# Reading x by column-tiled matmuls at the head of the second state visit, in an attention and gated FFN kernel

## The chip, the cores and the metric

The kernel runs on one core of a Trainium2 chip. The metric is the device time of one execution in microseconds (us). The core has a matrix engine (TensorE, PE in the profile, its weight loads PEld), a vector engine (VectorE, DVE), a scalar engine (ScalarE, ACT), a general one (GpSimd, POOL) and one that issues DMAs (SyncE, SP). Each takes its own list of instructions in order; they wait for each other by semaphores.

## The reference

There are 8 batches of 8 heads. In each head x has 512 rows and the state 32 rows, of 64 columns. x reads the state by softmax attention, and the state reads x; both results stand one under the other, and the 544 rows of a batch (heads side by side, 512 columns) go through a feed-forward layer with a gate.

```python
scores = scale * np.matmul(x, state.transpose(0, 1, 3, 2))
a = softmax(scores)                      # over the 32 state rows
xread = np.matmul(a, state)
scores2 = scale * np.matmul(state, x.transpose(0, 1, 3, 2))
a2 = softmax(scores2)                    # over the 512 rows of x
sread = np.matmul(a2, x)
x = np.concatenate([xread, sread], axis=2)       # to (8 * 544, 512)
gate = 1.0 / (1.0 + np.exp(-(x @ w_gate)))       # 512 -> 1536
out = (gate * (x @ w_val)) @ w_out               # 1536 -> 512
```

## The kernel before, in words

Everything is written out in order by hand (manual_schedule): an instruction stands in its engine's list where its call stands in the code. Matrices are bf16, sums float32.

For the rows of x the kernel doesn't form xread. It multiplies the state with the gate and value weights first (sw_wide, with sw_mm at L272: 64x32 tiles of the array, results in PSUM, copied to the tile SW by sw_cp at L310), and then multiplies the normalised attention (aT) with SW (gv_mm, L324). One batch has 12 steps f. Each step does four 512-column matmuls in gv_mm (two for the gate in one PSUM bank, two for the value in another), the tanh of the gate on ACT (gv_th, L334), the product of both on DVE (gv_glu, L339), and four matmuls of the output product of the batch before (out_mm, L355; every third ends a block, which ACT copies to res, L359, and SP writes out, L363).

The loop from L685 runs over b from 2 to 8. While batch b is in its gv_mm, the attention of batch nb = b + 1 is prepared, in the holes between:

- steps 0 and 6 (the two state visits, v = 0 and 1): sw_wide makes half of SW. Its first two results go to the banks OU (the output product's) and AT (the attention's), four more to the pool SWP. Then stands gv_mm of the step, then out_mm; in the other steps out_mm stands first;
- steps 1 and 2: S_mm (L136), the scores, into AT; S_exp (L141), their exponential E1, on ACT;
- steps 2 and 4: n_sum (L154, L156), the row sums and their reciprocals; steps 5 and 6: n_mul (L208), the attention product ab; step 6: aT_dma (L229), four transposing DMAs on SP's queue;
- step 3: at_Eb (L147), E1 as bf16 (Eb) on POOL; n_add (L173, L174) on DVE and p_fold (L182 to L193) on POOL, which add E1 up over the rows of x into hl;
- steps 9 and 10: the state reads x. sr_mm multiplies hl with the constant matrix pick (L241), which gives the sums, and then x with Eb: 16 matmuls (L249) with 128 columns of x (two heads) as weights and 64 columns of Eb moving. Half of the product (one head with the other's attention) isn't used. sr_inv (L254) takes the reciprocal of the sums on DVE, sr_fin (L262) multiplies and writes the columns of batch nb of XS;
- load_x (L75) for nb + 2 at step 0, cast_x (L99, POOL) and at_xT_dma (L123, SP) for nb + 1 at step 2. For nb = 3 some of it stands at steps 3 and 6.

The last pass, b = 8, multiplies the 256 rows in XS with the weights (L327) as batch 8. Batches 0 to 2 have their attention ahead of the loop, at L438 to L683, written out call by call, with sr_mm as above.

The pools for PSUM: AT one bank, OU one, GV two (gate and value, in turn), SWP four.

Of the kernel before, what the change touches and what calls it, by code (L numbers as in the profile page):

```python
# [8 lines left out]
FP = mybir.dt.float32  # L9
BF = mybir.dt.bfloat16  # L10
AF = mybir.ActivationFunctionType
ALU = mybir.AluOpType
# [4 lines left out]
def kernel(  # L17
# [14 lines left out]
    nc = tc.nc  # L32
    B, H, S, D = x.shape
    Ns = state.shape[2]
# [8 lines left out]
    wp = ctx.enter_context(tc.tile_pool(name="wp", bufs=1))  # L43
    stg = ctx.enter_context(tc.tile_pool(name="stg", bufs=3))
    xp = ctx.enter_context(tc.tile_pool(name="xp", bufs=2))
    ap_ = ctx.enter_context(tc.tile_pool(name="ap", bufs=2))
# [12 lines left out]
    wg = wp.tile((128, 4, dff), BF, name="wg")  # L59
    wv = wp.tile((128, 4, dff), BF, name="wv")  # L60
    wo = wp.tile((128, NF, 512), BF, name="wo")
    sTd = wp.tile((128, 2, H, 2, Ns), BF, name="sTd")
    XS = wp.tile((128, 4, B * Ns), BF, name="XS")

    AT, OU, GV, SWP = (p_at, "at"), (p_out, "outp"), (p_gv, "gv"), (p_sw, "swp")
    xfs, xhs, xbs, xTs = {}, {}, {}, {}
# [21 lines left out]
    def gate(landed):  # L88

        nc.gpsimd.tensor_copy(pre[:, 1:2], landed)  # L90
# [61 lines left out]
    def n_sum(b, i):  # L152
        rs = ap_.tile((128, 8, 2), FP, name="rs")
        nc.vector.tensor_reduce(rs, halfE(b, i), AX.X, ALU.add)  # L154
        ri = held["ri", b, i] = ap_.tile((128, 8, 2), FP, name="ri")
        nc.vector.reciprocal(ri, rs)  # L156
# [12 lines left out]
    def n_add(b):  # L169

        E2 = ap_.tile((128, 2, 2, 4, Ns), FP, name="E2", bufs=1)
        held["E4", b] = ap_.tile((128, 2, 4, Ns), FP, name="E4")
        nc.vector.tensor_tensor(E2, E1s[b][:, 0:2], E1s[b][:, 2:4], ALU.add)  # L173
        nc.vector.tensor_tensor(held["E4", b], E2[:, 0], E2[:, 1], ALU.add)  # L174
# [29 lines left out]
    def n_mul(b, i, eng, lo=0, n=4):  # L204
        if b not in abs_:
            abs_[b] = ap_.tile((128, 4, 2, 128), BF, name="ab")
        ri, ce = held["ri", b, i], slice(2 * lo, 2 * lo + 2 * n)
        eng.tensor_tensor(abs_[b].rearrange("p c e (j n) -> p (c e) j n", n=Ns)[:, ce, 2 * i:2 * i + 2],  # L208
                          halfE(b, i)[:, ce], ri[:, ce].unsqueeze(3).to_broadcast((128, 2 * n, 2, Ns)), ALU.mult)
# [26 lines left out]
    def sr_mm(b, place):  # L236
        Eb = Ebs[b]
        held["sr", b] = place[0].tile((128, 512), FP, name="srp", tag=place[1])
        sr, sm = sr_parts(b)
        if ("hl", b) in held:  # L240
            nc.tensor.matmul(sm, pick, held["hl", b], start=True, stop=True)  # L241
            terms = []
        else:
            terms = [(e, Eb[:, c, e]) for e in range(2) for c in range(4)]
        for i, (e, rhs) in enumerate(terms):
            nc.tensor.matmul(sm, ones[:, e], rhs, start=(i == 0), stop=(i == len(terms) - 1))
        for j in range(4):
            for c in range(4):
                nc.tensor.matmul(sr[:, j], xbs[b][:, c, 2 * j:2 * j + 2].rearrange("p h d -> p (h d)"),  # L249
                                 Eb[:, c, :, j], start=(c == 0), stop=(c == 3))  # L250

    def sr_inv(b):
        r2 = held["r2", b] = ap_.tile((128, 4, Ns), FP, name="r2")
        nc.vector.reciprocal(r2, sr_parts(b)[1])  # L254

    def sr_fin(b):
        if ("r2", b) not in held:
            sr_inv(b)
        sr, r2 = sr_parts(b)[0], held["r2", b]
        for e in range(2):  # L260
            rows = slice(e * 64, (e + 1) * 64)
            nc.vector.tensor_tensor(XS[rows, :, b * Ns:(b + 1) * Ns], sr[rows, :, e], r2[rows], ALU.mult)  # L262

    sw_left = {}

# [20 lines left out]
            for e in range(2):  # L288
                sw_left[b, lo, w, e] = (SWs[b][:, e, w, lo:lo + n], pss[e])

    def sw_wide(b, v):

        if b not in SWs:
            SWs[b] = fp.tile((128, 2, 2, dff), BF, name="SW", bufs=2)
        lo = 768 * v
        for k, places in enumerate(((OU, AT), (SWP, SWP), (SWP, SWP))):
            pss = [p[0].tile((128, 512), FP, name="swp", tag=p[1]) for p in places]
            if k < 2:
                sw_mm(pss, b, k, lo, 512, 0)
            else:  # L300
                for w in range(2):
                    sw_mm(pss, b, w, lo + 512, 256, 256 * w)
            for e in range(2):
                if k < 2:
                    sw_left[b, v, k, e] = (SWs[b][:, e, k, lo:lo + 512], pss[e])
                else:
                    sw_left[b, v, k, e] = (SWs[b][:, e, :, lo + 512:lo + 768], pss[e].rearrange("p (w n) -> p w n", w=2))

    def sw_cp(b, lo, w, e, cp):
        cp(*sw_left.pop((b, lo, w, e)))  # L310
# [5 lines left out]
    def gv_mm(b, f, place):  # L316
        n = n_of(b)
        fs = slice(f * 128, (f + 1) * 128)
        pss = []
        for w in range(2):  # L320
            ps = place[0].tile((128, 512), FP, name="gvp", tag=place[1])[:, :n]
            if b < B:
                for g in range(2):
                    nc.tensor.matmul(ps, SWs[b][:, g, w, fs], aTs[b][:, :, g], start=(g == 0), stop=(g == 1))  # L324
            else:
                for j in range(4):
                    nc.tensor.matmul(ps, (wg, wv)[w][:, j, fs], XS[:, j], start=(j == 0), stop=(j == 3))  # L327
            pss.append(ps)
        held["gv", b, f] = pss

# [15 lines left out]
    def out_mm(b, k, place=None):  # L346
        c, f0 = k // 3, (k % 3) * 4
        if b == 0:

            c, f0 = k // 6 * 2 + k % 2, k % 6 // 2 * 4  # L350
        if f0 == 0:
            place = place or (SWP if b == B else OU)
            ops[b, c] = place[0].tile((128, 512), FP, name="outp", tag=place[1])
        for f in range(f0, f0 + 4):
            nc.tensor.matmul(ops[b, c], glus[b][:, f, c * 128:(c + 1) * 128], wo[:, f],  # L355
                             start=(f == 0), stop=(f == NF - 1))
        if f0 == 8:
            res = fp.tile((128, 512), FP, name="res", bufs=4)
            nc.scalar.activation(res, ops[b, c], AF.Copy, scale=0.5)  # L359
            if b < B:  # L360
                n = 256 if b == B - 2 and c < 3 else 512
                for lo in range(0, 512, n):
                    nc.sync.dma_start(rows_of(b, c)[:, lo:lo + n], res[:, lo:lo + n])  # L363
            else:
                for i in range(4):
                    r0 = (4 * c + i) * SC + S
                    eng = nc.gpsimd if c == 1 and i > 1 else nc.sync
                    eng.dma_start(out[r0:r0 + Ns], res[i * Ns:(i + 1) * Ns])  # L368
# [313 lines left out]
    gate(xTs[2][:, 0, 3, 0:1])  # L682
    gv_glu(1, 5)  # L683

    for b in range(2, B + 1):  # L685
        nb = b + 1 if b + 1 < B else None
        for f in range(NF):

            v, q = divmod(f, 6)
            ahead = nb is not None and q == 0  # L690
            if ahead:
                sw_wide(nb, v)
                sw_cp(nb, v, 0, 0, act)
                sw_cp(nb, v, 0, 1, act)
            for first in (ahead, not ahead):
                if first:
                    gv_mm(b, f, SWP if b == B and f % 2 else GV)
                    gv_th(b, f)
                    gv_glu(b, f)
                elif b < B or f < 9:  # L700
                    out_mm(b - 1, f)
            if nb is not None:
                if f in (0, 8):
                    sw_cp(nb, v, 1, 0, vec)
                if q in (1, 3, 4):
                    k = max(q + 1, 3)
                    sw_cp(nb, v, k // 2, k % 2, act)
                if f in (1, 2):
                    S_mm(nb, f - 1, AT)
                    S_exp(nb, f - 1)  # L710
                elif f == 9:
                    sr_mm(nb, AT)
                    sr_inv(nb)
                elif f == 10:
                    sr_fin(nb)
                if f in (2, 4):
                    n_sum(nb, f // 2 - 1)
                elif f in (5, 6):
                    n_mul(nb, f - 5, nc.vector)
                if f == 3:  # L720
                    n_add(nb)
                    at_Eb(nb)
                    p_fold(nb)
                if f == (3 if nb == 3 else 0) and nb + 2 < B:
                    load_x(nb + 2, nc.sync)
                if f == 6:
                    aT_dma(nb)
                if f == (6 if nb == 3 else 2) and nb + 1 < B:
                    cast_x(nb + 1, pool, 0, 4)
                    cast_x(nb + 1, pool, 4, 4)  # L730
                    at_xT_dma(nb + 1)
# [33 lines left out]
```

## Time and profile before

| | |
|---|---|
| median of 3 runs | 225.42 us (224.99 to 225.9) |
| profiled execution | 224.94 us |
| its span | 223.2 us |
| mean granted TensorE clock | 0.999 |
| PE, share of the span | 97% |
| DVE | 60% |
| ACT | 58% |
| POOL | 35% |

The profile is one execution. Its parts are the busy time of each engine, the span in 40 slices, the chain of work that ended last (followed back from the last instruction to what released each step), and groups of instructions by line, with mean duration and the idle time before them. The trace behind it gives instructions in order of time: start, time that the group took, engine, line, operation, tiles, tile of the array where there is one (64*32), shape, count, and in brackets the idle time before it and who ended it. Durations of matmuls include their way through the array, so neighbours overlap; the distance between starts tells what each costs.

### The profile page before, as it was taken

The numbers are of one execution on the slowest core, as the hardware profiler recorded it, in microseconds if no ns is written. First come the engines' busy times: TensorE is split into PE (matmuls) and PEld (weight loads), VectorE is DVE, ScalarE is ACT, GpSimd is POOL, SyncE is SP. The second block draws the span as 40 slices with busy tenths as digits, with TensorE's granted clock in tenths as the row PEclk, the third lists the DMA queues.
The fourth block names the chain that finished last, engine by engine and source line by source line (L and its number), as shares of the span: only waits on it lengthen the run. The fifth ranks groups of instructions, "written<-read, shape, count | busy, mean of one in ns | idle before, by whom it ended". The sixth has DMA issues, their size and how long they took to land.

```text
span 223.2 us, 4814 instructions
## 1 busy us (share of the span) xinstructions
PE 215.4 (97%) x1843; PEld 109.9 (49%) x1843; DVE 133.2 (60%) x229; ACT 129.5 (58%) x243; POOL 79.1 (35%) x166
## 2 busy tenths in 40 slices
PE   8688999999999999999999999999999999999994
PEld 8553344544444544444545444445445444566843
DVE  3799897967476646765485558563857344322301
ACT  2598886269675557556765658476665444432410
POOL 7987487650048502821262316400560000000001
PEclk9999999999999999999999999999999999999999
DMA  6999999916693269425551315230122112111113
GB/s 97 180 205 264 228 179 169 264 39 167 148 345 109 59 162 263 119 55 167 182 122 37 106 53 113 56 101 13 47 73 71 48 56 68 69 47 50 47 38 103
DMA packets 38871, 26.32 MB, mean 118 GB/s; under 512 B 21089, under 2 KB 34529, under 8 KB 38849
## 3 DMA queue, kind: packets, MB, share of 16 engines
q1 hardware_dynamic: 29600, 17.64, 30.3%
q0 software_dynamic: 8960, 8.19, 21.1%
q8 instruction: 14, 0.23, 0.4%
q10 hardware_dynamic: 288, 0.20, 0.3%
q14 instruction: 9, 0.07, 0.1%
HBM read 18.35 MB, written 8.91 MB: 122 GB/s over the span
## 4 chain that ended last, share of the span: by engine, by line
PE 92%; DVE 6%; ACT 1%; issue 0%; DVEq 0%
PE outp L355 38%; PE gvp L324 36%; PE swp L272 5%; PE gvp L327 5%; PE warm L391 2%; PE srp L249 1%; PE Sp L136 1%; PE outp L377 1%; DVE ab L208 1%; DVE ab L166 1%; DVE glu L339 1%; DVE rs L154 1%; PE aTp L215 1%; DVE rs L160 1%; DVE xT L118 0%; PE stp L413 0%
## 5 line engine op out<-in xcount | busy, mean ns | idle before, releaser
L339 DVE SCALAR_TENSOR_TENSOR glu<-th,gvp 128x512 bf16<-128x512 f32 (+1 forms) x108 | 70.1, 657 | 70.8 <-ACT th L334 55.4
L355 PE MATMUL outp<-wo,glu 128*128 128x512 bf16 x396 | 98.1, 379 | 0.0
L324 PE MATMUL gvp<-aT,SW 128*128 128x512 bf16 x384 | 96.8, 379 | 0.1
L334 ACT ACTIVATE th<-gvp 128x512 f32<-128x512 f32 (+1 forms) x108 | 61.6, 576 | 59.2 <-PE gvp L324 48.2
L324 PEld LDWEIGHTS <-SW 128*128 128x128 bf16 x384 | 36.1, 98 | 45.0 <-issue 4.1
L355 PEld LDWEIGHTS <-glu 128*128 128x128 bf16 x396 | 37.5, 98 | 41.0 <-issue 0.4
L310 ACT CAST SW<-swp 128x512 bf16<-128x512 f32 x74 | 40.9, 586 | 3.5 <-PE swp L272 2.2
L147 POOL CAST Eb<-E 128x256 bf16<-128x256 f32 x32 | 11.6, 410 | 56.0 <-ACT E L141 56.0
L359 ACT ACTIVATE res<-outp 128x512 f32<-128x512 f32 x33 | 19.7, 598 | 18.3 <-PE outp L355 18.2
L368 POOL DMA_DIRECT2D out_dram<-res x2 | 1.1, 538 | 52.5 <-ACT res L359 52.5
L310 DVE CAST SW<-swp 128x512 bf16<-128x512 f32 x22 | 14.8, 684 | 2.5 <-PE swp L272 2.5
L99 POOL CAST xb<-xf 128x1024 bf16<-128x1024 f32 x9 | 9.1, 1041 | 14.0 <-issue 8.0
L141 ACT ACTIVATE E<-Sp 128x512 f32<-128x512 f32 x16 | 9.6, 604 | 1.7 <-PE Sp L134 1.4
L187 POOL COPY F<-G 32x128 f32<-32x128 f32 x28 | 9.9, 354 | 1.3
L208 DVE TENSOR_TENSOR ab<-E,ri 128x512 bf16<-128x512 f32 x12 | 9.0, 750 | 0.1
L182 POOL COPY F<-E 64x128 f32<-64x128 f32 x14 | 5.3, 378 | 10.5 <-DVE E L174 10.0
L272 PE MATMUL swp<-wg,sTc 64*32 64x512 bf16 (+1 forms) x192 | 8.4, 328 | 0.0
L154 DVE TENSOR_REDUCE rs<-E 128x16 f32<-128x512 f32 x12 | 8.2, 680 | 0.0
L272 PEld LDWEIGHTS <-sTc 64*32 64x32 bf16 x384 | 4.5, 91 | 7.3 <-issue 5.1
L254 DVE RECIPROCAL r<-srp 128x128 f32<-128x128 f32 x8 | 7.6, 951 | 0.2 <-PE srp L249 0.2
L272 PE MATMUL swp<-wv,sTc 64*32 64x512 bf16 (+1 forms) x192 | 7.4, 322 | 0.0
L327 PE MATMUL gvp<-XS,wg 128*128 128x256 bf16 x48 | 7.2, 273 | 0.0
(76 smaller groups left out, 153.1 us busy)
## 6 DMA issues: line engine op xcount, KB each, us to landing
out_dram<-res SPq DMA_DIRECT2D x28, 256.0 KB, 2.5
xf<-in_x_dram SPq DMA_DIRECT2D x4, 1024.0 KB, 6.7
xf<-in_x_dram POOLq DMA_DIRECT2D x2, 1024.0 KB, 11.7
wo<-in_moe_w_out_dram POOLq DMA_DIRECT2D x3, 512.0 KB, 9.3
xh<-in_x_dram POOLq DMA_DIRECT2D x4, 256.0 KB, 5.4
wg<-in_moe_w_gate_dram POOLq DMA_DIRECT2D x2, 512.0 KB, 10.1
wv<-in_moe_w_val_dram POOLq DMA_DIRECT2D x2, 512.0 KB, 11.3
out_dram<-res SPq DMA_DIRECT2D x7, 128.0 KB, 1.9
```

Of the source, the lines that this page charges most:

```text
L147: nc.gpsimd.tensor_copy(Ebs[b][:, c], E1s[b][:, c])
L154: nc.vector.tensor_reduce(rs, halfE(b, i), AX.X, ALU.add)
L187: pool(F[32 * q:32 * q + 32, 1], G[32 * r:32 * r + 32, 0])
L208: eng.tensor_tensor(abs_[b].rearrange("p c e (j n) -> p (c e) j n", n=Ns)[:, ce, 2 * i:2 * i + 2], halfE(b, i)[:, ce], ri[:, ce].unsqueeze ...
L272: nc.tensor.matmul(pss[e][j * Ns:(j + 1) * Ns, o:o + n], sTc[rows, b, j] if b > 1 else sTd[rows, b, 2 * j + e, e], (wg, wv)[w][rows, j, lo ...
L310: cp(*sw_left.pop((b, lo, w, e)))
L324: nc.tensor.matmul(ps, SWs[b][:, g, w, fs], aTs[b][:, :, g], start=(g == 0), stop=(g == 1))
L327: nc.tensor.matmul(ps, (wg, wv)[w][:, j, fs], XS[:, j], start=(j == 0), stop=(j == 3))
L334: nc.scalar.activation(th, held["gv", b, f][0], AF.Tanh, scale=0.5)
L339: nc.vector.scalar_tensor_tensor(glus[b][:, f], held["th", b, f], 1.0, held["gv", b, f][1], ALU.add, ALU.mult)
L355: nc.tensor.matmul(ops[b, c], glus[b][:, f, c * 128:(c + 1) * 128], wo[:, f], start=(f == 0), stop=(f == NF - 1))
L359: nc.scalar.activation(res, ops[b, c], AF.Copy, scale=0.5)
```

## The change

For batches 3 to 7 the state reads x in another way. Batches 0 to 2 keep theirs.

- rd_mm takes the place of sr_mm. It stands at the head of the second visit (step 6), ahead of sw_wide. It has 32 matmuls, for two head parities e, four row groups c and four head pairs j: 32 columns of Eb are the weights, and 64 columns of x and one column of ones move. Results for j go to partitions 32 j to 32 j + 31 of the bank AT. Column 65 holds the sums.
- x for this is in a new tile xs, with the ones set once ahead of the loop. cast_xs fills it on POOL at step 0, in two parts, behind a gate: a copy of one element that waits for the tanh of step 0.
- rd_fin (DVE, after sw_wide in step 6): reciprocal of two columns, one multiplication of 128 columns into xr. rd_dma (SP, after aT_dma): one transposing DMA of xr into XS. XS has the batch ahead of the head pair now, so its reader at the end takes eight pieces of 32 columns.
- n_add, p_fold, sr_mm, sr_inv and sr_fin go from the loop.
- The second visit's second bank comes from GV instead of AT. Its copy is then the first of the two on ACT.
- n_sum stands at steps 2 and 3, n_mul at step 4 and, for the second half, behind the visit in step 6, ahead of that step's product of gate and value.
- cast_x and at_xT_dma stand at step 1 instead of 2 (for nb = 3 still at 6).
- Rows of batch 5 are written in two halves each, as those of batch 6 were.

```diff
-    XS = wp.tile((128, 4, B * Ns), BF, name="XS")
+    XS = wp.tile((128, B, 4, Ns), BF, name="XS")
+    xs = wp.tile((128, 4, H, D + 2), BF, name="xs")
...
+    def cast_xs(b, lo, n):
+        pool(xs.rearrange("p c h d -> p h c d")[:, lo:lo + n, :, :D], xfs[b][:, lo:lo + n])
+
+    def rd_mm(b):
+        ps = AT[0].tile((128, 512), FP, name="rdp", tag=AT[1])
+        rd = held["rd", b] = ps[:, :2 * D + 2].rearrange("p (e d) -> p e d", e=2)
+        for e in range(2):
+            for c in range(4):
+                for j in range(4):
+                    nc.tensor.matmul(rd[j * Ns:(j + 1) * Ns, e], Ebs[b][:, c, e, j], xs[:, c, 2 * j + e, :D + 1],
+                                     start=(c == 0), stop=(c == 3))
+
+    def rd_fin(b):
+        rd = held["rd", b]
+        r2 = ap_.tile((128, 2, 1), FP, name="rr")
+        nc.vector.reciprocal(r2, rd[:, :, D:])
+        xr = held["xr", b] = ap_.tile((128, 2, D), BF, name="xr")
+        nc.vector.tensor_tensor(xr, rd[:, :, :D], r2.to_broadcast((128, 2, D)), ALU.mult)
+
+    def rd_dma(b):
+        nc.sync.dma_start_transpose(XS[:, b].rearrange("p j n -> p (j n)"), held["xr", b].rearrange("p e d -> p (e d)"))
...
-    def sw_wide(b, v):
+    def sw_wide(b, v, other=AT):
...
-        for k, places in enumerate(((OU, AT), (SWP, SWP), (SWP, SWP))):
+        for k, places in enumerate(((OU, other), (SWP, SWP), (SWP, SWP))):
...
-                    nc.tensor.matmul(ps, (wg, wv)[w][:, j, fs], XS[:, j], start=(j == 0), stop=(j == 3))
+                    nc.tensor.matmul(ps, (wg, wv)[w][:, j, fs], XS[:, :, j], start=(j == 0), stop=(j == 3))
...
-                n = 256 if b == B - 2 and c < 3 else 512
+                n = 256 if B - 4 < b < B - 1 and c < 3 else 512
...
+    nc.gpsimd.memset(xs[:, :, :, D:], 1.0)
...
-                sw_wide(nb, v)
-                sw_cp(nb, v, 0, 0, act)
-                sw_cp(nb, v, 0, 1, act)
+                if v:
+                    rd_mm(nb)
+                sw_wide(nb, v, GV if v else AT)
+                if v:
+                    n_mul(nb, 1, nc.vector)
+                    rd_fin(nb)
+                sw_cp(nb, v, 0, v, act)
+                sw_cp(nb, v, 0, 1 - v, act)
...
-                elif f == 9:
-                    sr_mm(nb, AT)
-                    sr_inv(nb)
-                elif f == 10:
-                    sr_fin(nb)
-                if f in (2, 4):
-                    n_sum(nb, f // 2 - 1)
-                elif f in (5, 6):
-                    n_mul(nb, f - 5, nc.vector)
+                if f in (2, 3):
+                    n_sum(nb, f - 2)
+                elif f == 4:
+                    n_mul(nb, 0, nc.vector)
                 if f == 3:
-                    n_add(nb)
                     at_Eb(nb)
-                    p_fold(nb)
...
                 if f == 6:
                     aT_dma(nb)
-                if f == (6 if nb == 3 else 2) and nb + 1 < B:
+                    rd_dma(nb)
+                if f == 0:
+                    gate(held["th", b, 0][:, 0:1])
+                    cast_xs(nb, 0, 4)
+                    cast_xs(nb, 4, 4)
+                if f == (6 if nb == 3 else 1) and nb + 1 < B:
```

More of the change, by code (lines that the diff above doesn't have):

```diff
@@ L261, in sr_fin @@
             rows = slice(e * 64, (e + 1) * 64)
-            nc.vector.tensor_tensor(XS[rows, :, b * Ns:(b + 1) * Ns], sr[rows, :, e], r2[rows], ALU.mult)
+            nc.vector.tensor_tensor(XS[rows, b], sr[rows, :, e], r2[rows], ALU.mult)
+    def cast_xs(b, lo, n):
[16 more added lines that the diff above has]
+        nc.sync.dma_start_transpose(XS[:, b].rearrange("p j n -> p (j n)"), held["xr", b].rearrange("p e d -> p (e d)"))
     sw_left = {}
```

## The prediction

> **What bounds the kernel now.** I read the shares by engine first, then the chain of work that ended last, then the stages of the span, cut at the first tiled matmul of successive batches.
>
> ```profile
> PE 215.4 (97%) x1843; PEld 109.9 (49%) x1843; DVE 133.2 (60%) x229; ACT 129.5 (58%) x243; POOL 79.1 (35%) x166
> PEclk9999999999999999999999999999999999999999
> PE 92%; DVE 6%; ACT 1%; issue 0%; DVEq 0%
> 55.44:78.91 23.47, 23.47 (x194) 11.02 (x193) 15.05 (x26) 14.93 (x29) 10.59 (x20) 1.00 0.60 165
> 78.91:102.40 23.49, 23.49 (x194) 10.95 (x193) 14.73 (x25) 15.00 (x29) 8.48 (x18) 1.00 0.63 146
> ```
>
> TensorE carries 92% of the chain, at full granted clock. In the two stages (length, then busy time of PE, PEld, DVE, ACT, POOL) it is busy for 23.47 of 23.47 us and 23.49 of 23.49 us, while DVE and ACT have a third of the time left and POOL more than half. So in the loop over batches an edit is worth exactly what it takes from or adds to TensorE's queue, unless it makes TensorE wait. The shorter lists of DVE and POOL (n_add, p_fold, the long reciprocal) earn nothing by themselves.
>
> **What it removes from TensorE.** In each of five batches, at step 9, sr_mm: one pick matmul and 16 products.
>
> ```profile
> 74.94 0.22 PE L241 MATMUL srp<-hl,pick 128*128 128x128 bf16 x1
> 75.00 0.63 PE L249 MATMUL srp<-Eb,xb 128*128 128x64 bf16 x16
> 75.46 1.03 PE L355 MATMUL outp<-wo,glu 128*128 128x512 bf16 x4
> ```
>
> Durations overlap, because matmuls are pipelined; what counts is from start to start. 75.46 - 74.94 = **0.52 us**; the 16 products take 0.46 us, 0.029 us each.
>
> **What it adds to TensorE.** rd_mm: 32 matmuls with 32 weight columns and 65 moving columns each. Four of them, one for each j, go to four column strips of the array, and eight such groups follow each other; then come the 64-row tiles of the visit. Before has no 128x32 tile. The nearest rows are sT_mm's (L413): 128 rows, 64 moving columns, two column strips, followed by the same visit matmuls.
>
> ```profile
> 28.60 1.03 PE L324 MATMUL gvp<-aT,SW 128*128 128x512 bf16 x4
> 29.55 0.32 PE L413 MATMUL stp<-ident,sb 128*64 128x64 bf16 x8
> 29.80 0.63 PE L272 MATMUL swp<-wg,sTd 64*32 64x512 bf16 x16
> 30.36 1.04 PE L324 MATMUL gvp<-aT,SW 128*128 128x512 bf16 x4
> 31.32 0.44 PE L413 MATMUL stp<-ident,sb 128*64 128x64 bf16 x16
> 31.69 0.63 PE L272 MATMUL swp<-wv,sTd 64*32 64x512 bf16 x16
> ```
>
> Eight of them (four pairs) hold TensorE for 29.80 - 29.55 = 0.25 us up to the next tile shape, sixteen (eight pairs) for 31.69 - 31.32 = 0.37 us: 0.03 us a pair and about 0.12 us for starting and changing shape. A pair of 64-column weights loads 128 weight columns, as do four 32-column weights, and 65 columns stream about as long as 64. Eight groups therefore cost what eight pairs do: **0.37 us**. The change into tiles (four 0.216 us matmuls from 28.60 end at 29.46, so 0.09 us) was paid by the visit already and stays.
>
> Bounds: from below, eight groups at 0.029 us with no further change of shape, 0.23 us; from above, 32 matmuls one after another, 32 x 0.029 + 0.10 = 1.03 us. I take 0.37 us, from the nearest row.
>
> Net in a batch: 0.37 - 0.52 = -0.15 us, if nothing waits.
>
> **The visit's banks.** Step 6 of batch 3 in before (the visit is L272):
>
> ```profile
> 89.76 1.03 PE L324 MATMUL gvp<-aT,SW 128*128 128x512 bf16 x4
> ...
> 90.45 0.59 ACT L334 ACTIVATE th<-gvp 128x512 f32<-128x512 f32 x1
> ...
> 90.72 0.41 PE L272 MATMUL swp<-wg,sTc 64*32 64x512 bf16 x8
> 90.94 0.40 PE L272 MATMUL swp<-wv,sTc 64*32 64x512 bf16 x8
> ...
> 91.08 0.69 DVE L339 SCALAR_TENSOR_TENSOR glu<-th,gvp 128x512 bf16<-128x512 f32 x1 [0.21 <-ACT th L334]
> ...
> 91.19 1.07 ACT L310 CAST SW<-swp 128x512 bf16<-128x512 f32 x2
> ...
> 91.49 0.55 PEld L324 LDWEIGHTS <-SW 128*128 128x128 bf16 x4 [0.21 <-issue]
> 91.49 1.04 PE L324 MATMUL gvp<-aT,SW 128*128 128x512 bf16 x4
> 91.68 0.76 DVE L208 TENSOR_TENSOR ab<-E,ri 128x512 bf16<-128x512 f32 x1
> ```
>
> In the changed kernel rd starts where the visit does now, 90.72, the visit at 91.09, gate(6) at 91.86, val(6) at 92.29, out_mm at 92.72. Each now waits for somebody else:
> - the visit's first matmuls need step 5's gate bank: th ends at 90.45 + 0.59 = 91.04, 0.05 us before;
> - gate(6) takes step 5's value bank: glu ends at 91.77, 0.09 us before;
> - val(6) takes the lent bank: the copy comes first on ACT now, 0.47 us after the visit starts (91.19 - 90.72), and takes 0.54 of 1.07 us: 92.10, 0.19 us before;
> - out_mm needs the second copy: 92.63, 0.09 us before.
>
> The one handing over that is shown, ACT to DVE (91.04 to 91.08), takes 0.04 us, so all four just pass. They also cap the gain: gate(6) cannot start before about 91.81, so a cheaper rd could not save more than 0.52 - (91.81 - 91.49) = 0.20 us in a batch. Behind a waiting gate(6) stands all of TensorE's queue; nothing else is late.
>
> **The other edits, costed at nothing.**
>
> ```profile
> 80.44 0.61 ACT L334 ACTIVATE th<-gvp 128x512 f32<-128x512 f32 x1
> 85.64 0.60 ACT L141 ACTIVATE E<-Sp 128x512 f32<-128x512 f32 x1
> 86.30 1.44 POOL L147 CAST Eb<-E 128x256 bf16<-128x256 f32 x4 [8.58 <-ACT E L141]
> L99 POOL CAST xb<-xf 128x1024 bf16<-128x1024 f32 x9 | 9.1, 1041 | 14.0 <-issue 8.0 <-PE gvp L324 4.1 <-PE srp L249 1.9
> L90 POOL CAST pre<-xT 128x1 f32<-128x1 bf16 x1 | 0.6, 581 | 0.1
> L254 DVE RECIPROCAL r<-srp 128x128 f32<-128x128 f32 x8 | 7.6, 951 | 0.2 <-PE srp L249 0.2
> L262 DVE TENSOR_TENSOR XS<-srp,r 64x128 bf16<-64x128 f32 x16 | 4.6, 286 | 0.2
> L156 DVE RECIPROCAL ri<-rs 128x16 f32<-128x16 f32 x12 | 3.0, 253 | 0.4
> 85.62 5.69 SPq L123 DMA_TRANSPOSE xT<-xb  x4
> 94.15 5.03 SPq L229 DMA_TRANSPOSE aT<-ab  x4
> ```
>
> POOL: the gate opens when th ends, 81.05; 0.58 us for it and four casts of 1.04 us end at 85.8. Eb then starts at 86.3 as now (its exponential decides) and ends at 87.74, three us before rd at 90.72. Without that cover each us would stop TensorE for a us. DVE: behind glu(5), to 91.77, stand n_mul (0.76), the reciprocal of two columns (at most 0.25) and the multiplication (about 0.29): 93.07, and glu(6) cannot start earlier than its th: ACT's two copies end at 92.63, th takes 0.6 more. So neither delays the other. The step-4 product falls on the time that n_sum leaves. SP: the xT transposes go out one step sooner, behind the casts (85.8, now 85.62), the four for aT right after n_mul, about 1.6 us sooner than 94.15, and rd_dma adds one issue of 5.03 / 4 = 1.26 us. Behind it stand writes of res, which has four buffers, and aT is needed at the next batch only (from 102.4, the end of the stage above), so the cover is whole; XS is read only after the last batch. The halved writes of batch 5 fall into the same slack.
>
> The last products read XS in eight pieces of 32 columns now.
>
> ```profile
> L327 PE MATMUL gvp<-XS,wg 128*128 128x256 bf16 x48 | 7.2, 273 | 0.0
> 61.74 0.40 PE L136 MATMUL Sp<-sTz,xT 128*128 128x64 bf16 x8
> 61.97 1.03 PE L355 MATMUL outp<-wo,glu 128*128 128x512 bf16 x4
> 194.46 0.60 PE L327 MATMUL gvp<-XS,wg 128*128 128x256 bf16 x4
> ```
>
> L249's moving operand is two pieces of 32 and takes 0.029 us; L136's is one of 64 and takes (61.97 - 61.74) / 8 = 0.029 us. Pieces cost nothing there: zero. Upper bound: the pairs above, with pieces of eight, take 0.031 us, 0.002 more for 64 columns; 0.008 for 256, times 96, is 0.8 us. A gain has no reason.
>
> **The sum.** Five batches x -0.15 = **-0.75 us** against the profiled execution's 224.94 us (span 223.2 and 1.7 around it): 224.2. The median of the three runs is 225.42, 0.48 above that execution, so the forecast is 224.7 us, 0.33% less. What a measurement can tell from no change is about 0.5%, 1.13 us; the cap above (5 x 0.20 = 1.0 us) lies within it.
>
> **The rivals.**
> - *Bank waits eat it.* If handing a bank to TensorE takes 0.1 us and not 0.04, the visit starts 0.05 us late and gate(6) 0.01 to 0.05 more. Left: -0.05 to -0.10 in a batch, 224.9 to 225.2. For it: margins of 0.05 and 0.09 us. Against: the same hand-overs occur at every step and TensorE shows no hole. Chance 0.17.
> - *TensorE's queue runs dry (slower).* Rd and visit are 64 short matmuls with their weight loads in 91.86 - 90.72 = 1.14 us, 0.018 us each. The densest stretch that before shows is this:
>
> ```profile
> 13.15:15.17 2.02, 1.92 (x65) 1.51 (x63) 1.65 (x4) 1.57 (x4) 1.07 (x3) 1.00 1.25 208
> ```
>
>   65 in 2.02 us, 0.031 each. If instructions came no faster, 64 would take 2.0 us: 0.9 us late, +0.75 net in a batch, +3.7 in all, 229.1. It decides once supply is slower than 0.018 us a matmul. Against it: the visit's 32 take 0.77 us in each batch without a hole; but 64 in a row are never shown. Chance 0.10. [...]
> - *The four strips don't overlap at 65 columns (slower).* 32 x 0.029 + 0.10 = 1.03 us, +0.51 in a batch, 228.0. For it: no row has four strips with so short a stream. Against: the visit's eight 512-column tiles take 90.94 - 90.72 = 0.22 us together, and L413's pairs overlap. Chance 0.06. [...]
> - *Rd waits for Eb or xs*, so that the order doesn't do what it says: three us of slack on POOL would have to go. Chance 0.04, 226 to 228.
> - *More than forecast*: rd at its lower bound and the cap reached, -1.0 us, 224.4, or scatter on top of it. Chance 0.08.
>
> **How the numbers follow.** The forecast itself keeps 0.55. Faster by over 0.5% needs scatter (the three runs reach 0.43 below their median) on the forecast or the last case: 0.08 + 0.07 = 0.15. Slower by over 0.5%: 0.10 + 0.06 + 0.04 = 0.20. Within: 0.65. Range: low 225.42 - 1.0 - 0.43 = 224.0, set to 223.9; high: no gain left and most of the 0.8 us bound on XS, 226.0. The two slow cases and late inputs, 0.20 together, stay outside.
>
> **What would show it.** In the profile after: from rd's first matmul to the visit's first 0.37 us; step 9 without sr; batch stages of 23.3 us, still full; no releaser on the visit or on gate(6). Wrong would be: rd's matmuls 0.03 us apart singly, visit matmuls that start late with no semaphore named, rd or the visit waiting on POOL, ACT or DVE, or L327's eight taking more than now.

## The result and the profile after

| | before | after |
|---|---|---|
| median | 225.52 us (224.99 to 225.9) | 224.38 us (223.8 to 224.72) |
| ratio to before, 95% interval | | 0.9949 [0.9931, 0.9966] |
| profiled execution, its span | 224.94, 223.2 us | 224.35, 222.6 us |

The change makes the kernel 0.51% faster, 1.14 us, where 0.75 us was forecast: 224.38 us for a forecast of 224.7 and a range of 223.9 to 226.0. The interval takes in 0.5%, below which the prediction calls a change not to be told from none.

The engines, the queue for instructions and the chain, on the page of after:

```profile
PE 214.1 (96%) x1895; PEld 110.0 (49%) x1918; DVE 123.3 (55%) x214; ACT 129.5 (58%) x243; POOL 64.7 (29%) x122
...
q14 instruction: 8, 0.07, 0.1%
...
PE 91%; DVE 5%; issue 1%; ACT 1%; DVEq 0%
```

TensorE still carries 91% of the chain. DVE gave back 10 us of work and POOL 14. Two batch stages of after, cut as those of before were (length; then busy time of PE, PEld, DVE, ACT, POOL):

```profile
56.14:79.46 23.32, 23.16 (x206) 10.87 (x208) 13.46 (x23) 14.93 (x29) 5.59 (x9) 1.00 0.62 166
79.46:102.79 23.33, 23.17 (x206) 10.79 (x208) 12.73 (x22) 15.00 (x29) 5.56 (x9) 1.00 0.69 150
```

A stage is 23.32 us where it was 23.47. The 0.16 us that PE lacks in each stage is no stall: some matmul records are missing in this trace. The groups of the output product show it, with 373 matmuls for 396 weight loads:

```profile
L379 PE MATMUL outp<-wo,glu 128*128 128x512 bf16 x373 | 95.4, 379 | 1.4 <-issue 0.3
L379 PEld LDWEIGHTS <-glu 128*128 128x128 bf16 x396 | 37.8, 98 | 42.2 <-issue 0.4
```

The new head of the second visit, step 6 of batch 3, in order of time in the trace of after:

```profile
90.23 1.03 PE L348 MATMUL gvp<-aT,SW 128*128 128x512 bf16 x4
...
90.92 0.59 ACT L358 ACTIVATE th<-gvp 128x512 f32<-128x512 f32 x1
...
91.19 0.42 PE L277 MATMUL rdp<-xs,Eb 128*32 128x65 bf16 x32
...
91.54 0.43 PE L296 MATMUL swp<-wg,sTc 64*32 64x512 bf16 x8
91.55 0.69 DVE L363 SCALAR_TENSOR_TENSOR glu<-th,gvp 128x512 bf16<-128x512 f32 x1 [0.49 <-ACT th L358]
91.77 0.42 PE L296 MATMUL swp<-wv,sTc 64*32 64x512 bf16 x8
...
92.04 1.07 ACT L334 CAST SW<-swp 128x512 bf16<-128x512 f32 x2 [0.52 <-PE swp L296]
...
92.16 0.69 DVE L209 TENSOR_TENSOR ab<-E,ri 128x512 bf16<-128x512 f32 x1
...
92.34 1.04 PE L348 MATMUL gvp<-aT,SW 128*128 128x512 bf16 x4
92.76 0.16 DVE L283 RECIPROCAL rr<-rdp 128x2 f32<-128x2 f32 x1
...
92.95 0.29 DVE L285 TENSOR_TENSOR xr<-rdp,rr 128x128 bf16<-128x128 f32 x1
```

The 32 matmuls of rd start at 91.19 and the visit at 91.54: 0.35 us (0.356 in the trace's finer times, the mean of the five batches). Gate(6), the L348 group at 92.34, comes 1.15 us after rd (finer: 1.153). The tanh ends at 91.52 in these times; DVE starts 0.03 us later. Not on these lines, since a group shows only its first start: the visit's first matmul into the lent bank starts 0.380 us after rd, 0.05 us after the tanh ended.

Where the time went, from the traces (us; stage: first visit to first visit):

| | start to loop | one stage | loop to last products | last matmul to end | span |
|---|---|---|---|---|---|
| before | 55.54 | 23.47 | 138.92 | 3.54 | 223.2 |
| before again | 56.06 | 23.47 | 138.92 | 3.55 | 223.7 |
| after | 56.16 | 23.323 | 138.11 | 3.15 | 222.6 |
| after again | 56.11 | 23.323 | 138.11 | 3.15 | 222.5 |

The last products on XS take 17.28 us in all four. The start scatters from 55.3 to 56.3 us over all the traces. Between the two kernels, 5 x 0.146 = 0.73 us lies in the batches, 0.08 us in a hole near 191 us, and 0.39 us behind the last matmul. These make 1.20 us; the medians give 1.14.

### The profile page after: what moved, and what is told of

It reads as the page before. It is cut to its first block, busy times and chain, and to the rows that moved or that the text cites. A ratio compares the mean times of both kernels' runs of the same rounds, so it can differ in the third digit from the quotient of the medians.

```text
span 222.6 us, 4895 instructions
## 1 busy us (share of the span) xinstructions
PE 214.1 (96%) x1895; PEld 110.0 (49%) x1918; DVE 123.3 (55%) x214; ACT 129.5 (58%) x243; POOL 64.7 (29%) x122
## 4 chain that ended last, share of the span: by engine, by line
PE 91%; DVE 5%; issue 1%; ACT 1%; DVEq 0%
PE outp L379 38%; PE gvp L348 36%; PE swp L296 5%; PE gvp L351 5%; PE warm L415 3%; PE Sp L137 1%; PE outp L401 1%; PE rdp L277 1%; DVE ab L167 1%; DVE ab L209 1%; DVE glu L363 1%; DVE rs L155 1%; PE aTp L216 1%; DVE rs L161 1%; DVE xT L119 0%
## 5 line engine op out<-in xcount | busy, mean ns | idle before, releaser
L348 PE MATMUL gvp<-aT,SW 128*128 128x512 bf16 x384 | 96.7, 379 | 0.1
L379 PE MATMUL outp<-wo,glu 128*128 128x512 bf16 x373 | 95.4, 379 | 1.4 <-issue 0.3
L348 PEld LDWEIGHTS <-SW 128*128 128x128 bf16 x384 | 36.1, 98 | 45.0 <-issue 3.9
L91 POOL COPY pre<-th 128x1 f32<-128x1 f32 x5 | 0.9, 187 | 73.4 <-ACT th L358 73.4
L268 POOL CAST xs<-xf 128x1024 bf16<-128x1024 f32 x10 | 10.2, 1043 | 0.0
L415 PE MATMUL warm<-ones 128*128 128x128 bf16 x68 | 6.6, 286 | 1.0 <-DVE ones L461 1.0
```

The source lines that it names most:

```text
L415: nc.tensor.matmul(ps[:, :128], ones[:, 0], ones[:, 0], start=True, stop=True)
```

## The experiments

The theory was the prediction's: in the loop the time is TensorE's queue, so the gain is sr's 0.52 us less rd's 0.37. The rivals were waits for banks, a queue that runs dry, strips in turn, and (once the result was there) a second gain outside the loop.

**Rd at step 9 (5 rounds).** Only the place of rd is undone, and with it the loan of the bank.

```diff
-                if v:
-                    rd_mm(nb)
-                sw_wide(nb, v, GV if v else AT)
+                sw_wide(nb, v)
                 if v:
                     n_mul(nb, 1, nc.vector)
-                    rd_fin(nb)
-                sw_cp(nb, v, 0, v, act)
-                sw_cp(nb, v, 0, 1 - v, act)
+                sw_cp(nb, v, 0, 0, act)
+                sw_cp(nb, v, 0, 1, act)
...
+                elif f == 9:
+                    rd_mm(nb)
+                    rd_fin(nb)
+                    rd_dma(nb)
...
-                    rd_dma(nb)
```

> The changed kernel with its 32 column-tiled matmuls moved to step 9, where the old read stood, among matmuls of the full array; the second visit has its old bank again. Theory (the gain is what goes from TensorE's list, and the head of the visit saves one change of array shape): rd now pays a change into tiles (0.09 us in before, 29.46 to 29.55) and out of them besides its eight groups, 0.09 + 0.37 = 0.46 us against 0.52, so a batch takes 23.41 us instead of 23.47 (before) and 23.32 (after), and the whole about 0.3 us less than before. Rival 'the place doesn't matter': 23.32 us a batch, 0.75 us less than before. Rival 'relief' (DVE and POOL, freed of n_add and p_fold, carry the gain): as after, too.

Measured: 224.75 us, 0.9975 [0.9963, 0.9987]; a stage of 23.41 us. TensorE around rd in this kernel:

```profile
97.51 1.03 PE L348 MATMUL gvp<-aT,SW 128*128 128x512 bf16 x4
98.46 0.43 PE L277 MATMUL rdp<-xs,Eb 128*32 128x65 bf16 x32
```

Four matmuls of 0.216 us from 97.51 end at 98.37: 0.09 us to change into tiles. The stage is 0.06 us shorter than in before, so of sr's 0.52 us rd takes 0.46 here, as expected: this 0.09 and 0.37. So of 0.146 us in a batch, the place at the visit's head, where that change of shape was paid already, makes 0.09, and the narrower matmuls make the rest. The whole fell by 0.5 to 0.6 us and not by the 0.3 expected, since the end, 3.17 us, is after's.

**The lent bank alone (3 rounds).** Before, with GV's bank in the second visit (sw_wide takes the other bank as an argument, as in the change).

```diff
...
-                sw_wide(nb, v)
-                sw_cp(nb, v, 0, 0, act)
-                sw_cp(nb, v, 0, 1, act)
+                sw_wide(nb, v, GV if v else AT)
+                sw_cp(nb, v, 0, v, act)
+                sw_cp(nb, v, 0, 1 - v, act)
```

> The kernel before with one part of the change alone: the second visit takes one of the two gate and value banks, and that bank's copy is first on ACT. Nothing stands ahead of the visit. Theory: the visit's matmuls into the lent bank wait for step 5's tanh (its end is 0.32 us after the visit's start now), and gate(6) waits for step 5's glu, which ends at 91.77 where gate(6) starts at 91.49 now; with 0.05 us of handing over that is 0.33 us a batch, 23.80 us, and 1.7 us in all (about 227.2). Rival: another bank costs nothing, because TensorE has enough to do: 23.47 us a batch, 225.5.

Measured: 226.98 us, 1.0073 [1.0056, 1.009]; a stage of 23.846 us. TensorE in step 6:

```profile
91.11 0.79 PE L272 MATMUL swp<-wg,sTc 64*32 64x512 bf16 x8
91.52 0.60 PE L272 MATMUL swp<-wv,sTc 64*32 64x512 bf16 x8
...
92.27 1.04 PE L324 MATMUL gvp<-aT,SW 128*128 128x512 bf16 x4
```

The matmuls on wg go in turn to the bank OU and to the lent bank. The visit's second one, the first for the lent bank, starts 0.38 us after the first by the finer times, 0.05 us after the tanh ended, and all that stands behind it is as late: those on wv start 0.41 us after the first on wg; in before it was 0.22. Gate(6) comes 92.27 - 91.11 = 1.16 us after the visit starts (finer: 1.153), the same as from rd in after. Lending the bank alone costs 0.376 us a batch, where 0.33 was expected; in after, rd stands in that wait. 23.846 less sr's 0.52 is 23.33: a stage of after.

**Strips in turn (3 rounds).** Does the speed of rd come from four neighbouring matmuls that go to four strips?

```diff
-            for c in range(4):
-                for j in range(4):
+            for j in range(4):
+                for c in range(4):
```

> The changed kernel with two loops of rd_mm exchanged: the four matmuls that add up in one column strip follow each other, then the next strip. The work is the same. Theory: rd is cheap because four strips stream at once; in this order only the last of a strip overlaps the first of the next, so each half takes (4 x 3 + 1) x 0.029 = 0.38 us instead of 0.12, rd some 0.76 instead of 0.25: +0.5 us a batch, 23.83 us, and about 2.6 us in all against after (227.0). Rival 'the strips don't overlap anyway, matmuls this short cost 0.008 us each whatever their place': 23.32 us and 224.4.

Measured: 224.44 us, 0.9957 [0.9942, 0.9972]; a stage of 23.336 us. The theory fell:

```profile
91.30 0.46 PE L277 MATMUL rdp<-xs,Eb 128*32 128x65 bf16 x32
91.69 0.41 PE L296 MATMUL swp<-wg,sTc 64*32 64x512 bf16 x8
```

Rd takes 0.39 us up to the visit, 0.034 more, and the stage grows by 0.013 only, since the visit no longer waits for the lent bank. Four matmuls on one strip behind each other don't cost 4 x 0.029 us. What makes it so was not tried further, so why rd is cheap stays open.

**Rd twice (5 rounds).** The same 32 matmuls stand twice (work is added, results are those of the second pass): the price of rd with no wait ahead of the visit, and 96 short matmuls in a row.

```diff
-        for e in range(2):
+        for e in (0, 1, 0, 1):
```

> The changed kernel with the 32 matmuls of rd issued twice; the second pass writes the same values again. Theory: eight more groups of 0.031 us; the waits of 0.02 us for the banks go, since the visit starts later: +0.23 us a batch, 23.55 us, +1.15 in all, so about 225.5, the time of before. Rival 'TensorE's list runs dry': 96 short matmuls in a row, 0.014 us each, need more than is supplied; holes with no semaphore named appear in rd or the visit, and a batch takes 23.8 us or more (32 x 0.031 = 1.0 us late at the worst).

Measured: 225.36 us, 0.9997 [0.9984, 1.0011]; a stage of 23.567 us.

```profile
90.88 0.69 PE L277 MATMUL rdp<-xs,Eb 128*32 128x65 bf16 x64
91.50 0.41 PE L296 MATMUL swp<-wg,sTc 64*32 64x512 bf16 x8
...
92.28 1.04 PE L348 MATMUL gvp<-aT,SW 128*128 128x512 bf16 x4
```

64 matmuls take 0.62 us up to the visit, and the visit 0.78: 96 in 1.40 us, 0.015 each, with no hole. Sixteen groups less eight are 0.62 - 0.356 = 0.26 us, 0.033 a group, so some 0.1 us of rd is its start and change of shape.

**No row sums (5 rounds).** Before, without the sums of the second softmax in batches 3 to 7 (n_add, p_fold left out; a part of Eb stands in for hl).

```diff
-                    n_add(nb)
                     at_Eb(nb)
-                    p_fold(nb)
+                    held["hl", nb] = Ebs[nb][:, 0, 0].rearrange("p j n -> p (j n)")
```

> The kernel before without n_add on DVE and p_fold on POOL in batches 3 to 7; the pick matmul takes a part of Eb in place of the sums. It leaves out the row sums of the second softmax there. TensorE's list is the same. Theory: DVE and POOL are not what a batch waits for: 23.47 us a batch and 225.5 us, as before. Rival 'relief': most of the change's gain, about 23.35 us a batch and 224.6 to 224.9.

Measured: 224.9 us, 0.9979 [0.9966, 0.9991]. The stages are 23.47 us as in before (one of them 23.53), so in the batches the sums were indeed free. But the last matmul is followed by 3.10 us only, and the hole near 191 us is gone. The shorter lists earn 0.4 to 0.5 us elsewhere.

**Half of rd (5 rounds).** One head parity is left out of rd; the other's result stands for both.

```diff
-        for e in range(2):
+        for e in range(1):
...
-        nc.vector.reciprocal(r2, rd[:, :, D:])
+        nc.vector.reciprocal(r2, rd[:, 0:1, D:].to_broadcast((128, 2, 1)))
...
-        nc.vector.tensor_tensor(xr, rd[:, :, :D], r2.to_broadcast((128, 2, D)), ALU.mult)
+        nc.vector.tensor_tensor(xr, rd[:, 0:1, :D].to_broadcast((128, 2, D)), r2.to_broadcast((128, 2, D)), ALU.mult)
```

> The changed kernel with half of rd: 16 matmuls, for one of the two parities of the heads; the other half's result is left out and a copy of the first stands in its place. Theory: four groups less would be 0.12 us a batch, but the visit then stands at th's end and gate(6) at glu's: gate(6) starts 1.15 us after rd now and glu(5) ends 1.05 us after rd's start, so with 0.05 us of handing over at most 0.05 us is gained, 23.27 us a batch, 0.25 us in all. Rival 'the bank waits don't bind': 23.20 us a batch and 0.6 us in all.

Measured: 224.26 us, 0.9945 [0.9926, 0.9965]; a stage of 23.323 us, that of after.

```profile
91.02 0.30 PE L277 MATMUL rdp<-xs,Eb 128*32 128x65 bf16 x16
91.25 0.55 PE L296 MATMUL swp<-wg,sTc 64*32 64x512 bf16 x8
91.48 0.54 PE L296 MATMUL swp<-wv,sTc 64*32 64x512 bf16 x8
...
92.17 1.04 PE L348 MATMUL gvp<-aT,SW 128*128 128x512 bf16 x4
```

The visit starts 0.23 us after rd, but gate(6) again 1.15 us after it (finer: 1.153): the visit now takes 0.92 us, because the lent bank comes when the tanh is done (its first matmul there starts 0.380 us after rd, as in after, and 0.05 us after the tanh's end). After stands at the limit that the bank sets, and a cheaper rd gains nothing.

**After and before again (5 and 3 rounds, unchanged).** Was the excess over 0.75 us the scatter of the start?

> The changed kernel once more, to see how much of the time changes from run to run outside the loop: 23.32 us a batch. Theory: the loop gives 0.75 to 0.8 us, so the ratio to before is 0.9965, and what the median showed beyond it (1.14 us) is scatter of the part ahead of the loop (0.62 us later in after's trace) and of the end (0.39 us shorter). Rival: a second gain lies outside the loop, in the end, and the ratio is 0.995 again, with the last matmul to the end of the span at 3.15 us and not 3.54.

> The kernel before once more, as a run with a profile of its own: 23.47 us a batch, ratio 1.000. Theory: the part ahead of the loop and the end vary as much here as between before and after (start to the loop's first visit 55.5 to 56.2 us; last matmul to the end 3.1 to 3.6 us). Rival: both stand at before's values, 55.5 and 3.54, within 0.1 us.

Measured: after 224.35 us, 0.9947 [0.9929, 0.9966]; before 225.54 us, 1.0011 [0.9994, 1.0029]. The start of before came to 56.06 us, so it scatters, as the theory had it. The end stayed: 3.55 us in before and 3.15 in after, in the table above. The second gain is there in both traces of each kernel.

The end, then. DVE's last copy in before, in after (second fence), and two of the DMA queues in the window from 218 us to the end of each (others are left out):

```profile
219.88 0.29 DVE L383 TENSOR_SCALAR res<-outp 128x128 f32<-128x128 f32 x1 [0.92 <-PE outp L377]
```

```profile
219.68 0.29 DVE L407 TENSOR_SCALAR res<-outp 128x128 f32<-128x128 f32 x1 [0.92 <-PE outp L401]
```

```profile
q10 hardware_dynamic: 144, 0.07, 3.5%
q14 instruction: 1, 0.01, 0.4%
```

```profile
q10 hardware_dynamic: 144, 0.07, 3.5%
```

From that copy to the end of the span are 3.28 us in before and 2.89 in after. Before (third fence) loads a packet of instructions there on q14, after (fourth) none. The kernels' lists for POOL have 202 instructions in before, 163 in after, 139 in the run without row sums (the traces record 201, 162 and 138 of them). That gave a theory: instructions are loaded in blocks, and in before POOL steps into a new block at its very last. It says that only the length of POOL's list matters, and was tried both ways, with instructions that do nothing of use (small fills that stand in the last pass and run between 158 and 169 us, where POOL is idle: ahead of its last two issues it has 59.74 us of idle time in after and 52.49 in before).

**After, POOL's list longer (5 rounds).**

```diff
+            if b == B and f == 1:
+                for _ in range(39):
+                    nc.gpsimd.memset(pre[:, 1:2], 0.0)
```

> The changed kernel with 39 memsets of one column added to POOL's list at the start of the last pass, where POOL is idle; its list has 202 instructions, as many as in before (163 in after). New theory for what the loop doesn't explain (the 0.39 us between the last matmul and the end, 3.54 in before, 3.15 in after): the length of POOL's list decides whether a block of instructions has to be fetched while the core closes; the trace of before shows an 8 KB instruction packet at 223.17, that of after none behind 205.55. So the end is 3.54 us again, with such a packet, and the whole is 0.39 us more than after (ratio to before 0.9964). Rival 'less work on POOL': idle time is only filled, 3.15 us, ratio 0.9947.

Measured: 224.8 us, 0.9967 [0.9954, 0.998]; the end 3.60 us, stages and the rest as in after. DVE's last copy, and the same two queues in the same window:

```profile
219.64 0.29 DVE L407 TENSOR_SCALAR res<-outp 128x128 f32<-128x128 f32 x1 [0.92 <-PE outp L401]
```

```profile
q10 hardware_dynamic: 144, 0.07, 3.5%
q14 instruction: 1, 0.01, 0.5%
```

The packet is back, and 3.34 us from the copy to the end (223.0).

**Before, POOL's list longer still (5 rounds).** The same with 20 fills, in before (222 instructions).

> The kernel before with 20 such memsets, 222 instructions on POOL's list: more work. Theory of the list's length: the place at which the next block is needed moves 20 instructions ahead of the close, into idle time, and the end takes 3.15 us: faster than before by 0.39 us (ratio 0.9983), though only work was added; the batches stay at 23.47 us. Rival 'less work on POOL' or 'the end belongs to the old read': 3.54 us, ratio 1.000.

Measured: 224.85 us, 0.9979 [0.9968, 0.999]; the end 3.12 us. Work was only added, and the kernel is 0.5 us faster:

```profile
219.65 0.29 DVE L383 TENSOR_SCALAR res<-outp 128x128 f32<-128x128 f32 x1 [0.91 <-PE outp L377]
```

```profile
q10 hardware_dynamic: 144, 0.07, 3.5%
```

Now 2.86 us lie between the copy and the end (222.5), and no packet: by the theory the block is loaded earlier. The window from 160.5 to 162 us, in which before has nothing on q14, holds a packet in this trace (at 161.27):

```profile
q14 instruction: 1, 0.01, 2.4%
```

The place of the loss can be seen on POOL itself. Near its end its list has three instructions named DRAIN, and the second of them, at 222 us, differs; its duration is the middle one of the three. POOL's drains in before, in after, in after with 39 fills and in before with 20 (shortest, middle and longest in ns):

```profile
L760 POOLq DRAIN  x3: 46/235/3207, 218.6 to 222.9; - x3
L788 POOLq DRAIN  x3: 46/93/3202, 218.4 to 222.3; - x3
L791 POOLq DRAIN  x3: 46/236/3251, 218.3 to 222.7; - x3
L763 POOLq DRAIN  x3: 46/102/3188, 218.3 to 222.2; - x3
```

By the trace's finer times that drain also starts 0.36 us after the instruction ahead of it in the first and the third, and 0.06 in the others. With its longer duration that is 0.44 us, nearly all of the 0.45 us by which 39 fills lengthen the end of after. All four traces with 201 recorded instructions on POOL show it (before, before again, the lent bank, after with 39 fills), and none of the other nine. Two things in the theory are not shown. The packet, at 223.17 us in before, starts 0.72 us after that drain began and 0.1 us after POOL's last instruction ended, so its transfer isn't what POOL waits for. And in before with 20 fills the instruction at the same place of the list, the 197th recorded, is a fill, and starts no later than its neighbours.

**After, DVE's list longer (5 rounds).** The hole near 191 us by the same reasoning: DVE's list has 359 instructions in before and 343 in after. Sixteen fills bring it to 359 again.

```diff
+    spare = wp.tile((128, 2), FP, name="spare")
...
+            if nb is not None and (f > 8 or (b, f) == (2, 7)):
+                nc.vector.memset(spare, 0.0)
```

> The changed kernel with 16 memsets of two columns added to DVE's list in steps 9 to 11 of the loop (and one in step 7 of the first batch); 359 instructions as in before (343 in after). Theory of the list's length: the hole of 0.08 us in TensorE's list that before shows 0.3 us ahead of an 8 KB instruction packet (191.36) comes back between the loop's last visit and the products of the last pass, and first visit to first L327-product takes 138.19 us and not 138.11; the end stays at 3.15; the whole is within 0.1 us of after. Rival: no hole, 138.11.

Measured: 224.16 us, 0.995 [0.9933, 0.9967]; in the trace the last part is 0.07 us longer and the hole is there again. (From the first visit to the last products it is 138.32 us, where 138.19 was expected; the other 0.14 lies in the first stage, see below.) DVE and TensorE in before, in after and in this kernel:

```profile
188.79 0.69 DVE L339 SCALAR_TENSOR_TENSOR glu<-th,gvp 128x512 bf16<-128x512 f32 x1 [1.09 <-ACT th L334]
190.70 0.69 DVE L339 SCALAR_TENSOR_TENSOR glu<-th,gvp 128x512 bf16<-128x512 f32 x1 [1.22 <-ACT th L334]
190.93 1.11 PE L324 MATMUL gvp<-aT,SW 128*128 128x512 bf16 x4
```

```profile
188.68 0.69 DVE L363 SCALAR_TENSOR_TENSOR glu<-th,gvp 128x512 bf16<-128x512 f32 x1 [1.10 <-ACT th L358]
190.35 0.69 DVE L363 SCALAR_TENSOR_TENSOR glu<-th,gvp 128x512 bf16<-128x512 f32 x1 [0.98 <-ACT th L358]
190.81 1.03 PE L348 MATMUL gvp<-aT,SW 128*128 128x512 bf16 x4
```

```profile
190.41 0.69 DVE L363 SCALAR_TENSOR_TENSOR glu<-th,gvp 128x512 bf16<-128x512 f32 x1 [1.21 <-ACT th L358]
190.65 1.09 PE L348 MATMUL gvp<-aT,SW 128*128 128x512 bf16 x4
```

Two products of gate and value lie 1.91 us apart in before and 1.67 in after: DVE comes 0.24 us late, and most of that is TensorE's slack, so 0.08 is left. The longer list brings back the long idle time (1.21 us), a packet on q14 at 191.4 us, and a TensorE group of 1.09 us in place of 1.03. The median shows nothing of it: 0.07 us is within its scatter.

The traces say more than the hole does. The late product is the 320th instruction that the trace records of DVE in before, and in all thirteen traces the 320th is the late one. With 357 recorded it falls into the loop, 0.25 to 0.28 us after the tanh that releases it, where its neighbours take 0.03. In after, with 341, it falls into the last pass. There, in after (first fence), it stands after 1.67 us of idle time where its neighbours have 1.31; in this kernel (second fence) the same product is in time:

```profile
204.44 0.42 DVE L363 SCALAR_TENSOR_TENSOR glu<-th,gvp 128x256 bf16<-128x256 f32 x1 [1.67 <-ACT th L358]
```

```profile
203.99 0.42 DVE L363 SCALAR_TENSOR_TENSOR glu<-th,gvp 128x256 bf16<-128x256 f32 x1 [1.31 <-ACT th L358]
```

So the shorter list doesn't remove the delay. It moves it to a place where TensorE doesn't feel it: the last products take 17.28 us with and without it. A packet on q14 follows in each trace, 0.65 to 1.2 us after the late product starts, so here too it comes after the delay.

One thing was not foreseen: the first stage is 0.137 us longer, because a product of n_mul in batch 3 takes 1.47 us (1.17 in after) and the next glu comes late. POOL's casts run beside it; that they cause it is only argued.

## Why the prediction was right, and where its sum was short

- *TensorE's queue is the price in the loop:* right. Sr out, rd in: -0.146 us a batch against -0.15; rd up to the visit 0.356 us against 0.37; five batches 0.73 us against 0.75.
- *The pairs of L413 as the row for rd:* right in size. Rd twice gives 0.033 us a group and 0.1 for start and change, where the row gave 0.03 and 0.12. The reason given, four strips that stream at once, is not shown: with four matmuls in a row on one strip rd takes 0.034 us more.
- *The banks:* the visit's margin of 0.05 us wasn't there. The lent bank makes the visit's second matmul wait 0.02 us, since ACT hands over to TensorE in 0.05 us and not 0.04 and rd is a little shorter. It costs gate(6) 0.02 us: 1.153 from rd, where 0.356 and the visit's 0.777 make 1.133. Val(6) and out_mm don't wait: they start 0.44 and 0.87 us after gate(6) in before and in after. The cap was put too far off: at most 0.20 us a batch, where half of rd shows that 0.146 is all. It was worked out from the end of the product (glu), but the lent bank comes first: from the tanh's end 0.05 us to the visit's first matmul there, and 0.77 more of visit up to gate(6).
- *POOL, SP and DVE hide their edits:* right; no releaser of theirs appears on rd, the visit or gate(6).
- *XS in pieces at nothing:* right, 17.278 and 17.277 us.
- *"The shorter lists of DVE and POOL (n_add, p_fold, long reciprocal) earn nothing by themselves":* **this step failed.** It is true of busy time in the batches (the run without row sums has stages of 23.47 us). But the shorter list of POOL takes 0.39 us off the end, and the shorter list of DVE moves a delay out of the loop, where it left a hole of 0.08 us on TensorE. The prediction counted what the instructions do, and not how many stand in a list. The lengthened lists show it in both directions for POOL (3.60 and 3.12 us), and for DVE in the traces alone.
- *The rivals:* the queue running dry (229.1) and the strips that don't overlap (228.0) fell with 96 matmuls in 1.40 us. Bank waits took 0.02 us a batch, and did not eat the gain down to 0.05 or 0.10. "More than forecast" came true in its time (224.4), for another reason than a cheaper rd: that the measured time met this case's number is luck. The 0.15 for a gain of over 0.5% rested on scatter and on a cheaper rd, and the 0.51% came from neither.

What lies under the failed step is told by the traces only in part: a delay at one place of a list (0.44 us on POOL at the end, 0.24 us on DVE), and behind it a packet of 8 KB on q14. What the engine waits for there stays open. The traces show that instructions come in packets, and of what size: on q14 8 of them make 0.07 MB in after, about 8 KB each. For DVE the place is the 320th recorded instruction, in all thirteen traces. For POOL no count is shown: lists of 163 and 222 keep clear of the end and 202 doesn't.

## What to carry to other kernels

Where one engine is full (here TensorE, busy for 23.47 of 23.47 us of a stage in before), cost an edit by the distance between starts on that engine, and put short tiled matmuls next to others of tiled shape: that place was worth more here (0.09 us a batch) than the narrower matmuls (0.06). A wait that another edit makes can hold new work for nothing (here the 0.376 us a batch that the lent bank costs alone hold the 0.356 us of rd), but then it is also the limit of what is gained. Differences below half a per cent may come from the length of an engine's list (0.45 us of 224.35 here): before crediting an idea with them, look at the instruction packets near the end and near single holes, and add or take away idle instructions in one run. Such a delay may only have moved.

## What was not expected of the hardware

- Twenty added instructions make a kernel 0.5 us faster (0.9979 [0.9968, 0.999]), and 39 make another 0.45 us slower (224.8 for 224.35), by the length of POOL's list alone.
- 128x32 tiles with 65 moving columns pass at 0.033 us for four, and the order of the strips changes 32 of them by 0.034 us in all.
- The 320th recorded instruction of DVE is late in all thirteen traces, wherever in the kernel it falls.
- The time from the start of the span to the loop differs by 0.7 us between executions whose code ahead of the loop is the same (55.33 to 56.06 us in five traces with before's, 55.56 to 56.26 in eight with after's). TensorE's first matmuls, 56 on the tile warm, are part of it: their group took 4.91 us in before and 5.75 in after, in the two traces below. It is not all, for before again has 4.66 us there and comes to its loop later than before:

```profile
1.04 4.91 PE L391 MATMUL warm<-ones 128*128 128x128 bf16 x56 [1.04 <-DVE ones L437]
```

```profile
1.04 5.75 PE L415 MATMUL warm<-ones 128*128 128x128 bf16 x56 [1.04 <-DVE ones L461]
```
